# A linear-attention and MoE kernel on one core: exclusive sums by subtraction, some transposes by DMA, the first weight matrix in four loads, and a new order

## The chip, the cores and the metric

The kernel runs on one core of a Trainium2 chip. The metric is the time of one execution on the device, in microseconds (us), lower is better. Most executions of one kernel agree within a per cent or so. An execution more than 1.5% above the fastest of the same kernel is called slow, and only fast ones are compared. TensorE does matmuls (its weight loads are listed apart and run beside the matmuls), VectorE (DVE), ScalarE (ACT) and GpSimd (POOL) do elementwise work, and the queue of SyncE (SP) issues most of the DMAs.

## The reference

Two operations in a row. The first is a linear attention with a decay per channel and a bonus u for the current token; the second is a two-layer MLP with a tanh gelu (called MoE here, with one expert).

```python
# r, k, v, w: (4, 8, 768, 48); u: (8, 48); w_in: (384, 2048); w_out: (2048, 384)
state = zeros((B, H, D, D))
for t in range(S):
    cur = einsum('bhd,bhe->bhde', u[None] * k_t, v_t)
    y[:, :, t] = einsum('bhd,bhde->bhe', r_t, state + cur)
    state = w_t[:, :, :, None] * state + einsum('bhd,bhe->bhde', k_t, v_t)
x = y.transpose(0, 2, 1, 3).reshape(B * S, H * D)
h = x @ w_in
g = 0.5 * h * (1 + tanh(c * (h + 0.044715 * h**3)))      # c = sqrt(2 / pi)
out = g @ w_out
```

## The kernel before

The sequence is cut into 12 units (3 windows of 256 tokens by 4 batches); a partition holds a pair of tokens, and one unit has two chunks of 64 pairs. A unit goes through: loads of r, k, v, w; logarithm of w; cumulative sums on TensorE; exponentials; scaling of k and r; their transposes; the scores (tiles mt, then masked into sc); y; the state; the MoE matmuls h and o. All of it is laid out by hand: one long string of words is the program order of every engine at once. A word is a step, with the unit, the PSUM banks after @, and the engine as the last letter.

```python
ORDER = """
const.3.D load.w.0 clr.S.1.D ... ln.2 cum.2@35 kw.2.P y.1.0@24 ... load_wout.0 ... rka.2.P ...
"""

def cum(q, e):                       # units 2 to 11
    lw = logws[q % NLW]
    z = bank([P, 512], FP, f"z{q}")
    PE.matmul(z[:, 0:HD], incl, lw[:, :, 0:D], start=True, stop=True)     # inclusive sum
    ...                              # 4 small matmuls: the sum of a whole chunk
    x = bank([P, 512], FP, f"x{q}")
    PE.matmul(x[:, 0:HD], strict, lw[:, :, 0:D], start=True, stop=True)   # exclusive sum
    st["z", q], st["x", q] = z, x

def Td(q, wh, e):                    # transposes of kk (wh 0) and rq (wh 1) by DMA, most units
    src = (kks[q % NKK], rqs[q % NRQ])[wh]
    dst = buf(f"T{wh}", q, 2, [P, 2, G, 2, 64], BF)
    for c2 in range(2):
        SP.dma_start(out=dst[:, c2]..., in_=src[ds(64 * c2, 64)]..., transpose=True)

def X(q, c2, e):                     # MoE input: 3 transposes per chunk, through a permutation
    ...                              # that also puts the two tokens of a pair back in order
    for cb in range(NCB):
        PE.transpose(st["Xp", q][:, c2, cb, :], xt[:, ts(cb, P)], perm...)

def Xc(q, e):                        # and their evacuation from PSUM
    t = buf("xT", q, 2, [P, 2, NCB, P], BF)
    ...

def mm1(q, i, e):                    # h: 6 matmuls of 256 columns
    ...
    w_t = w_in_sb[i * NWI // 8][:, cb, ds(i * 2 * P % (DF // NWI), 2 * P)]
    w_t = w_t.rearrange("p (m s) -> p s m", s=WOP)[:, f, :]     # WOP = 2: every second column

def gl(q, i, e):
    t = buf(f"g{i}", q, NG, [P, 2, WIN], BF)
    ACT.activation(out=t, in_=st.pop(("h", q, i)), func=AF.Gelu_apprx_tanh)
```

## Time and profile before

| | before |
|---|---|
| median of the three runs at the start | 183.63 us (182.74 to 185.92; the highest is slow) |
| span of the profiled run | 181.3 us |
| first h matmul at | 23.1 us |
| from the start of the first h matmul to the end of the last o matmul (the body) | 154.5 us |
| from there to the end (the tail) | 3.7 us |

The three parts are read from the matmuls in the trace. The prediction below shows the page and the chain of this run; two rows of the page's groups of instructions complete it. A row reads: line, engine, operation, output<-input, shape, count, then busy time in us and mean duration in ns, then the idle time of the engine before them.

```profile
L566 ACT ACTIVATE g<-h 128x512 bf16<-128x512 f32 x96 | 52.2, 600 | 24.7 <-PE h L560 24.1
L560 PEld LDWEIGHTS <-w_in_sb 128*128 128x128 bf16 x576 | 55.6, 98 | 9.5
```

All 96 gelus take 600 ns, the weight load of h takes 98 ns, and ScalarE idles before gelus because it waits for TensorE, not the other way round.

### The profile page before, as it was taken

The numbers are of one execution on the slowest core, as the hardware profiler recorded it, in microseconds if no ns is written. First come the engines' busy times: TensorE is split into PE (matmuls) and PEld (weight loads), VectorE is DVE, ScalarE is ACT, GpSimd is POOL, SyncE is SP. The second block draws the span as 40 slices with busy tenths as digits, with TensorE's granted clock in tenths as the row PEclk, the third lists the DMA queues.
The fourth block names the chain that finished last, engine by engine and source line by source line (L and its number), as shares of the span: only waits on it lengthen the run. The fifth ranks groups of instructions, "written<-read, shape, count | busy, mean of one in ns | idle before, by whom it ended". The sixth has DMA issues, their size and how long they took to land.

```text
span 181.3 us, 5364 instructions
## 1 busy us (share of the span) xinstructions
PE 175.4 (97%) x2237; PEld 128.9 (71%) x2237; DVE 106.7 (59%) x218; ACT 118.5 (65%) x221; POOL 111.1 (61%) x115
## 2 busy tenths in 40 slices
PE   7999899999999999999999999999999999999991
PEld 4367689866786698767866777867856776887660
DVE  3279996644689853583598885385094876720010
ACT  2679688774777698686973788865864924344721
POOL 8599899568989597527999999955066400000000
PEclk9999999999999999999999999999999999999999
DMA  5999999999999996999899885687754453021004
GB/s 148 261 261 238 262 232 233 247 248 235 213 173 208 277 204 96 269 275 248 81 278 297 169 232 105 175 189 84 189 150 87 79 93 113 0 86 48 0 22 151
DMA packets 73753, 31.53 MB, mean 174 GB/s; under 512 B 68865, under 2 KB 72962, under 8 KB 73730
## 3 DMA queue, kind: packets, MB, share of 16 engines
q1 hardware_dynamic: 71152, 27.08, 69.9%
q0 software_dynamic: 1856, 3.15, 9.4%
q10 hardware_dynamic: 722, 0.98, 1.6%
q8 instruction: 17, 0.28, 0.7%
q14 instruction: 6, 0.05, 0.1%
HBM read 25.17 MB, written 4.72 MB: 165 GB/s over the span
## 4 chain that ended last, share of the span: by engine, by line
PE 88%; POOL 3%; DMA 3%; DVE 1%; issue 1%; ACT 1%; SPq 1%; POOLq 0%
PE o L573 35%; PE h L560 35%; PE mt L459 4%; DMA k<-in_k_dram 3%; PE y L481 3%; PE y L524 2%; PE p L494 2%; PE Xp L541 2%; POOL rk L403 2%; PE z L323 1%; PE x L328 1%; POOL rk L409 1%; PE T L380 1%; DVE sc L466 1%; PE dummy L276 1%
## 5 line engine op out<-in xcount | busy, mean ns | idle before, releaser
L573 PE MATMUL o<-w_out_sb,g 128*128 128x384 bf16 x384 | 73.0, 326 | 0.0
L560 PE MATMUL h<-xT,w_in_sb 128*128 128x256 bf16 x576 | 69.5, 273 | 0.0
L566 ACT ACTIVATE g<-h 128x512 bf16<-128x512 f32 x96 | 52.2, 600 | 24.7 <-PE h L560 24.1
L560 PEld LDWEIGHTS <-w_in_sb 128*128 128x128 bf16 x576 | 55.6, 98 | 9.5
L573 PEld LDWEIGHTS <-g 128*128 128x128 bf16 x384 | 35.5, 98 | 18.5
L466 DVE CAST_PREDICATED sc<-mask,mt 128x512 bf16<-128x512 uint16 x48 | 30.0, 685 | 15.4 <-PE mt L459 15.3
L420 POOL TENSOR_TENSOR sc<-eye,dg 128x512 bf16<-128x512 bf16 x20 | 20.7, 1044 | 15.1 <-DVE dg L414 15.0
L403 POOL TENSOR_TENSOR rk<-k,u_bc 128x768 f32<-128x768 f32 x12 | 21.8, 1816 | 2.3 <-DMA k<-in_k_dram 2.2
L409 POOL TENSOR_TENSOR rk<-rk,r 128x768 f32<-128x768 f32 x12 | 21.8, 1818 | 0.2
L414 DVE TENSOR_REDUCE dg<-rk 128x16 f32<-128x768 f32 x12 | 11.4, 950 | 9.4 <-POOL rk L409 9.3
L582 DVE COPY ob<-o 128x384 f32<-128x384 f32 x11 | 6.1, 555 | 16.6 <-PE o L573 16.5
L515 DVE TENSOR_TENSOR s<-p,al 64x192 bf16<-64x192 f32 x40 | 14.2, 354 | 2.9 <-PE p L494 2.0
L353 POOL TENSOR_TENSOR rw<-r,w 128x384 f32<-128x384 f32 x10 | 10.0, 1001 | 8.8 <-DMA r<-in_r_dram 8.8
L531 ACT ACTIVATE xs<-y 128x384 bf16<-128x384 f32 x20 | 9.5, 489 | 8.0 <-PE y L524 5.4
L507 DVE TENSOR_TENSOR p<-p,s 64x192 f32<-64x192 f32 x32 | 11.7, 367 | 3.8 <-PE p L494 2.8
L580 ACT ACTIVATE ob<-o 128x384 f32<-128x384 f32 x13 | 6.4, 492 | 9.1 <-PE o L573 8.2
L281 POOL TENSOR_TENSOR ww<-w 128x384 f32<-128x384 f32 x10 | 10.0, 1005 | 2.4 <-DMA w<-in_w_dram 2.3
L347 POOL TENSOR_TENSOR kw<-k,w 128x384 f32<-128x384 f32 x10 | 10.0, 1003 | 2.5 <-DMA k<-in_k_dram 2.5
L630 ACT ACT_TABLE_LOAD x8 | 10.3, 1283 | 1.4 <-PEq L647 1.3
L632 ACT ACT_TABLE_LOAD x8 | 10.3, 1283 | 0.1
L276 PE MATMUL dummy<-warm_src 128*128 128x256 bf16 x41 | 7.3, 329 | 1.2 <-DVE warm_src L221 1.1
L432 POOL CAST vb<-v 128x768 bf16<-128x768 f32 x9 | 7.4, 823 | 1.6 <-DMA v<-in_v_dram 1.6
(90 smaller groups left out, 183.7 us busy)
## 6 DMA issues: line engine op xcount, KB each, us to landing
w<-in_w_dram SPq DMA_DIRECT2D x12, 384.0 KB, 5.2
k<-in_k_dram SPq DMA_DIRECT2D x12, 384.0 KB, 6.2
r<-in_r_dram SPq DMA_DIRECT2D x12, 384.0 KB, 6.4
v<-in_v_dram SPq DMA_DIRECT2D x12, 384.0 KB, 5.8
out_dram<-ob SPq DMA_DIRECT2D x19, 192.0 KB, 3.7
w_in_sb<-in_moe_w_in_dram POOLq DMA_DIRECT2D x2, 768.0 KB, 9.1
w_out_sb<-in_moe_w_out_dram POOLq DMA_DIRECT2D x2, 768.0 KB, 9.8
out_dram<-ob ACTq DMA_DIRECT2D x5, 192.0 KB, 2.3
```

The lines of the kernel that those rows point to most:

```text
L403: ENG[e].tensor_tensor(out=t, in0=st["k", q].rearrange("p h (t d) -> p h t d", t=2), in1=u_bc[:, :, None, :].broadcast_to([P, H, 2, D]), o ...
L409: ENG[e].tensor_tensor(out=t, in0=t, in1=st["r", q].rearrange("p h (t d) -> p h t d", t=2), op=AL.mult)
L414: DVE.tensor_reduce(out=t, in_=st.pop(("rk", q)), axis=AX.X, op=AL.add)
L420: POOL.tensor_tensor(out=bass.AP(tensor=o.tensor, offset=o.offset, ap=[list(o.ap[0]), [256, 4], [192, 2], [1, 64]]), in0=eye[:, None, None ...
L466: DVE.copy_predicated(scs[q % NSC][n][:, :, j].rearrange("p a b c i -> p a (b c i)"), mask.rearrange("p a b t -> p (a b t)").bitcast(U16)[ ...
L507: DVE.tensor_tensor(out=p2[rows, :, cols], in0=p2[rows, :, cols], in1=s[rows, :, cols], op=AL.add)
L515: DVE.tensor_tensor(out=s[rows, :, cols], in0=p2[rows, :, cols], in1=st["al", q][rows, :, c2][:, :, None].broadcast_to([64, G, D]), op=AL. ...
L560: PE.matmul(h[:, f, :], w_t, xt[:, :, cb, :], start=(f + cb == 0), stop=(cb == NCB - 1), skip_group_check=True)
L566: ACT.activation(out=t, in_=st.pop(("h", q, i)), func=AF.Gelu_apprx_tanh)
L573: PE.matmul(st["o", q, c2], st["g", q, i][:, f, ts(c2, P)], w_out_sb[i * NWO // 8][:, (2 * i + f) % (NFT // NWO), :], start=(i + f == 0), ...
L630: ACT.preload_act_table_set(EXP_SET)
L632: ACT.preload_act_table(AF.Gelu_apprx_tanh)
```

## The change

Four things at once. For units 2 to 11 the exclusive sum is no longer a matmul but the inclusive sum minus its own last term, on VectorE. For units 7, 9, 10 and 11 the MoE input is transposed by DMA; the DMA transpose used here does not permute tokens, so the gelu of those units writes its output in a strided order. w_in comes in four DMAs instead of two, and the weights' column step grows from 2 to 4. The same constant, WOP, also sets how many rows of w_out lie side by side in a partition, so that load changes too: its packets are 1024 of 1536 bytes before and 512 of 3072 after. The order string is new throughout.

```diff
-NWI = 2
+NWI = 4
-WOP = 2
+WOP = 4
+XSUB = 1
 ... (ORDER: all words in a new sequence; one place that matters later:)
-... kw.2.P ... load_wout.0 ... rka.2.P ...
+... rka.2.P ... load_wout.0 ... kw.2.P ...
 ... (in cum:)
-        x = bank([P, 512], FP, f"x{q}")
-        PE.matmul(x[:, 0:HD], strict, lw[:, :, 0:D], start=True, stop=True)
-        st["z", q], st["x", q] = z, x
+    def xd(q, e):
+        x = bank([P, 512], FP, f"x{q}")
+        DVE.tensor_tensor(out=x[:, 0:HD].rearrange("p (h d) -> p h d", d=D),
+                          in0=st["z", q][:, 0:HD].rearrange("p (h d) -> p h d", d=D),
+                          in1=logws[q % NLW][:, :, 0:D], op=AL.subtract)
+        st["x", q] = x
 ...
+    def Xd(q, c2, e):
+        if ("xT", q) not in st:
+            st["xT", q] = buf("xT", q, 2, [P, 2, NCB, P], BF)
+        SP.dma_start(out=st["xT", q][:, c2], in_=st.pop(("xs", q, c2)), transpose=True)
+        by_dma.add(q)
 ... (in gl:)
-        ACT.activation(out=t, in_=st.pop(("h", q, i)), func=AF.Gelu_apprx_tanh)
+        h = st.pop(("h", q, i))
+        if q in by_dma:
+            ACT.activation(out=t.rearrange("p f (c i s) -> p (f c) s i", c=2, s=2),
+                           in_=h.rearrange("p f (c s i) -> p (f c) s i", c=2, s=2),
+                           func=AF.Gelu_apprx_tanh)
+        else:
+            ACT.activation(out=t, in_=h, func=AF.Gelu_apprx_tanh)
```

## The prediction

> **What bounds the kernel now.** I read four things in this order: the engine shares and slices of the page, the waits of TensorE, the chain of work that ended last, and the groups by line. First the page:
>
> ```profile
> PE 175.4 (97%) x2237; PEld 128.9 (71%) x2237; DVE 106.7 (59%) x218; ACT 118.5 (65%) x221; POOL 111.1 (61%) x115
> PE   7999899999999999999999999999999999999991
> DMA  5999999999999996999899885687754453021004
> ```
>
> TensorE is busy 97% of the span, and every slice between the first five and the last is full. A busy TensorE is not proof of a full one, since the ends of matmuls are modelled and overlap, so I look at what it waited for. Its own list of waits is two lines long:
>
> ```profile
> PE dummy L276 <- DVE warm_src L221: 1.1, 1, 1.1
> PE y L524 <- issue: 0.5, 1, 0.5
> ```
>
> Both lie in the first 21 us. Later no matmul waits for another engine. The chain says the same in time order:
>
> ```profile
> 1.86 5.77 DMA k<-in_k_dram
> 7.78 1.82 POOL rk L403
> ...
> 15.63 1.21 DVE sc L466 x2
> 16.88 1.05 PE dummy L276 x8
> ...
> 22.99 0.28 PE y L524 x4
> 23.27 1.31 PE h L560 x12
> ...
> 152.45 0.17 PE Xp L541 x3
> ...
> 154.76 1.31 PE h L560 x12
> ...
> 169.46 8.14 PE o L573 x50
> 177.59 0.02 issue
> 177.62 0.49 ACT ob L580
> ```
>
> There are three parts. A head of 23.3 us to the first real MoE matmul runs through load, GpSimd and VectorE, and TensorE fills it with dummy matmuls. A body of 154.3 us is TensorE matmul after matmul. A tail of 3.7 us follows: the copy of 0.49 us, the store and the close. The chain also gives the true rates, which the mean durations hide: 12 h matmuls of 256 columns in 1.31 us are 109 ns each, 3 Xp transposes of 128 columns in 0.17 us are 56 ns. The 50 o matmuls of 384 columns in 8.14 us are 163 ns each. The rows that the change touches, by form:
>
> ```profile
> L541 PE MATMUL Xp<-perm,xs 128*128 128x128 bf16 x72 | 6.5, 219 | 0.0
> L328 PE MATMUL x<-logw,strict 128*128 128x384 bf16 x10 | 3.2, 322 | 0.0
> ```
>
> Their busy sums (6.5 and 3.2 us) overstate them about twofold: a mean of 219 ns holds a pipeline latency that the next matmul overlaps.
>
> **What the Trainium skill says.** "TensorE: Matmul & The Clock Gate", section "Back-to-back issue gap", gives N/2.4 + 2.5 ns for the isolated warm gap of N columns: 56, 109 and 163 ns for 128, 256 and 384. The trace agrees with all three. The same page, "Weight-path perf modes", says that the fast weight load of 128 non-fp32 weights allows a column step of up to about a thousand elements. The change reads w_in with a step of 4 where before it was 2; this trace has a mean load of 98 ns at step 2 and also at step 1 (g), and none at step 4. "VectorE: DVE Perf Modes", "The perf-mode tier table", puts a tensor_tensor with an operand in PSUM at 1x, so 384 columns are 384/0.96 = 400 ns and some set-up; the trace has 0.55 us for rq and kk of that shape. "DMA: Bandwidth & Descriptors", "Issuing engines are not separate DMA queues", says that all issuers share the same 16 engines; I use it for the loads of the head, where the DMA row stands at 9.
>
> **The change, part by part.**
> 1. Exclusive sums. For units 2 to 11 the strict matmul goes: 10 x 163 ns = 1.63 us off the body (unit 2's stands in the head, so 9 of them, 1.47 us, are certain). In its place VectorE subtracts logw from z: 10 x 0.55 us = 5.5 us on an engine that is at 59%. Exp of x now waits for z, then for the subtraction, so rq is some 0.5 us later per unit, and z in PSUM is held longer. The searched order puts other matmuls in between.
> 2. Transposes by DMA for units 7, 9, 10 and 11: 4 x 6 x 56 ns = 1.34 us of TensorE go, and with them four evacuations of 0.56 us (VectorE) or 0.81 us (ScalarE). Eight DMA transposes come in on SP. The existing ones occupy SP for about 1.26 us each and land after a median 3.0 us; each moves 128 KB, the new ones 98 KB, so about 1 us and 3 us. SP has room after 100 us, where the DMA row falls to 7 and below. Adding the rates above along the new order of TensorE, the slack for unit 11 is about 12 us of matmuls between the last a5 and mm1, for a path of 0.6 + 0.6 + 3 us; unit 9 has about 3 us after its second transpose. I see no stall there.
> 3. The gelu write with a stride of two elements: 32 of 96 gelus. Same element count, so I keep 0.60 us each; even 0.75 would add 4.8 us to a ScalarE at 65%.
> 4. w_in in four DMAs, the first some 6 us earlier: in the before trace a w_in half is issued at 11.89 us and lands 9.1 us later. The same bytes in all. Each quarter takes about 2 us of the DMA engines, estimated from the first half's roughly 4 us burst at 15 to 19 us. The first quarter now falls among the loads of k and r of unit 1.
> 5. The head. VectorE sets it: from its first evacuation of T at 11.6 us it works almost without a pause up to the decay of s at 22.7 us, which releases the last y and then h. The changed head has the same VectorE operations there. It can start about 0.5 us earlier, since unit 0's evacuation no longer follows a longer chain of exps, but k of unit 1 now comes at about 12.5 us by the load rates (1.5 us per load, plus the quarter of w_in), which takes it back. I count 0 to +0.5, say +0.2 us. Five more dummies (46 for 41) lie in idle time.
> 6. The tail: the last copy and store stay on ScalarE. Three other copies and two stores stand ahead of them there now, at 0.49 and 0.34 us; counted back from the last o matmul they just fit. 0 us.
>
> Sum: -1.6 - 1.3 + 0.2 = -2.7 us. I add 0.2 us for waits that a new order has on a chip and not on paper. With 183.6 before, that gives **181.1 us**, a gain of 1.4%.
>
> **The rivals.**
> - A new wait in the body, because rq comes later and the loads have been reordered (v of unit 3 now comes behind two transposes on SP). For it: the DMA row is at 9 through half the span, and one load issue held SP for 5.1 us. Against it: TensorE has 10 us and more of MoE matmuls of units 0 and 1 to run while unit 2 and 3 are prepared, and before shows no such wait. It would give 182 to 184 us.
> - The head grows, because w_in quarters and loads collide: the first h would start at 24.5 to 25.5 and take back half of the gain, 182 to 183.5 us. For it: the software queue takes most of the DMA bandwidth while it runs. Against it: the first half's worth of w_in is no longer ahead of r of unit 2.
> - The weight load at step 4 is slower than 109 ns and becomes the bound of 576 matmuls: 20 ns more each would be 11 us, about 192 us. For it: only 11 ns lie between 98 and 109. Against it: step 1 and step 2 cost the same 98 ns, and the skill's limit is far off.
> - The new order is also better elsewhere: the 1.1 us and 1.4 us that h and o take beyond their rates in the body go, and the head shortens by 0.5. That would be 179 us. The body has no more than these 2.5 us to give, as nothing in it waits.
>
> **Range and chances.** The part that I trust is the 2.7 to 3.0 us of TensorE work. Head and waits are uncertain by a microsecond to each side, more upward, as a saturated TensorE leaves little downward; the times before spread over 182.7 to 185.9. So 8 times in 10 within **179.4 to 183.4 us**. Faster by over 2% is a time under about 180.0 (or under 179.6, if the runs before come out as the lower two did), which needs the last rival in part: 0.2. Slower by over 2% needs the third rival, or a stall of over 6 us: 0.03. Within 2%: 0.77.
>
> **What would show it.** Right: TensorE loses 10 strict matmuls and 24 transposes, h keeps 109 ns and its weight load 98 ns, TensorE's list of waits stays empty after the first h, the first h starts at 22.8 to 24 us, and the body shortens to about 151.5 us; the gelus with the strided write stay at 0.60 us. Wrong: waits of TensorE for DMA, VectorE or ScalarE in the body, a first h after 24.5 us, a weight load over 105 ns, or a tail over 4 us. If the time falls under 179.5 us with a body of over 151 us, the head gave more than I allow.

## The result and the profile after

| | before | after |
|---|---|---|
| median, first pair of runs | 183.38 us (6 runs, one of them slow) | 181.41 us (6 runs, one of them slow) |
| ratio, fast runs | 1 | 0.9899, 95% interval 0.9869 to 0.9928 |
| the same kernels again in a later batch | 183.63 us (11 runs, two slow) | 182.95 us (6 runs, one slow) |
| ratio there | 1 | 0.9954, 0.9911 to 0.9997 |
| profiled run: span | 181.3 us | 180.1 us |
| profiled run: first h, body, tail | 23.1, 154.5, 3.7 us | 23.4, 153.1, 3.7 us |

A ratio is the mean time of one kernel's fast runs over the mean of the other's fast runs of the same rounds, so it is not quite the ratio of the medians quoted beside it. By the 2% measure the two kernels are the same; the change gains about 0.7% (the mean of 0.990 and 0.995), or 1.4 us. Where a text below says "the changed kernel's 0.993", it is this mean.

The page of the changed kernel, the lines that answer to those shown of before:

```profile
PE 172.5 (96%) x2208; PEld 134.0 (74%) x2208; DVE 112.1 (62%) x232; ACT 131.6 (73%) x225; POOL 112.7 (63%) x115
...
PE   7998999999999999999997999999899999999991
...
L578 PEld LDWEIGHTS <-w_in_sb 128*128 128x128 bf16 x576 | 62.1, 114 | 3.9
...
L590 ACT ACTIVATE g<-h 128x512 bf16<-128x512 f32 x64 | 34.7, 606 | 4.6 <-PE h L578 3.6
...
L586 ACT ACTIVATE g<-h 128x512 bf16<-128x512 f32 x32 | 21.6, 766 | 15.0 <-PE h L578 15.0
...
L654 ACT ACT_TABLE_LOAD x13 | 16.7, 1283 | 1.5 <-PEq L671 1.3
```

TensorE lost 2.9 us of busy time and 29 instructions net (10 matmuls and 24 transposes fewer, 5 dummies more). Two slices of its row in the body, which were full, are now at 7 and 8. ScalarE went from 118.5 to 131.6 us: the strided gelus take 766 ns instead of about 606, and there are 26 loads of activation tables (13 in the row shown and 13 in one beside it) where before had 16. The Trainium skill, "ScalarE: Activation LUTs", section "What ACT_TABLE_LOAD costs", gives about 1283 ns for one such load, which the trace shows to the nanosecond; ten more are 12.8 us. The loads were not foreseen, the slower gelus only as a fallback. Neither set the end in this run: ScalarE still idles before these gelus because TensorE has not made h yet.

The waits of TensorE in the changed kernel (who waited <- for whom: us in all, times, longest):

```profile
PE mt L471 <- DMA T<-rq: 1.1, 2, 0.9
...
PE p L506 <- POOL vb L444: 0.6, 1, 0.6
```

The kernel before had no wait in the body. These two are in it. The chain of waits around them shows where each comes from (start, duration, what; SPq is the issue of a DMA):

```profile
91.73 5.37 DMA T<-rq
...
97.15 0.64 PE mt L471 x31
...
118.37 1.27 SPq L408
...
119.74 0.53 SPq L249
...
120.31 5.92 DMA v<-in_v_dram
...
126.36 0.83 POOL vb L444
...
127.23 0.50 PE p L506 x8
```

The DMA transpose of rq of unit 7 is issued at 91.7 us and takes 5.4 us to land; the scores wait for it. Later, v of unit 10 is issued at 120.3 us, after the issue of four transposes has held SyncE one behind the other from 113.6 to 119.6 us (the 1.27 us of SPq is the last of them) and the issue of another load another 0.5 us. It lands 5.9 us later, is cast by GpSimd, and only then the p matmuls run.

The gaps between starts of matmuls, less the rate of each kind, are 1.05 us and 0.40 us at the first place and 0.73 us at the second: 2.2 us. Nine strict matmuls and 24 transposes in the body are 9 x 163 + 24 x 56 ns = 2.8 us less work. The body is 1.4 us shorter. So the rest of the new order won 1.4 - (2.8 - 2.2) = 0.8 us. By the same count of gaps, 0.4 us of it is in the intervals after h matmuls, which run closer to their rate; those after o matmuls do not, and the rest lies among the small matmuls.

The first of these waits is not the work of the new DMA transposes. In the time line of SyncE the first of them is issued at 105.9 us, when the scores of unit 7 have already waited at 96.7 us. The place of unit 7's own transposes in the new order is the likelier cause: e1 and e2 below move one of them, and the wait for rq goes (but it is missing from the one profiled run of e3 too, which moves nothing). The old order missed the same wait narrowly: the last transpose of unit 7 landed at 103.1 us there, and its scores began at 103.5 us. Before the load of v of unit 10, two new transposes do stand in the queue (105.9 and 111.7 us).

### The profile page after: what moved, and what is told of

Read it like the earlier page. It is cut to its first block, busy times and chain, and to the rows that moved or that the text cites. A ratio compares the mean times of both kernels' runs of the same rounds, so it can differ in the third digit from the quotient of the medians.

```text
span 180.1 us, 5345 instructions
## 1 busy us (share of the span) xinstructions
PE 172.5 (96%) x2208; PEld 134.0 (74%) x2208; DVE 112.1 (62%) x232; ACT 131.6 (73%) x225; POOL 112.7 (63%) x115
## 4 chain that ended last, share of the span: by engine, by line
PE 85%; DMA 6%; DVE 3%; SPq 1%; issue 1%; ACT 1%; POOL 0%; POOLq 0%
PE o L597 33%; PE h L578 30%; DMA v<-in_v_dram 3%; PE mt L471 3%; DMA T<-rq 3%; PE y L493 3%; PE dummy L279 3%; PE p L506 2%; PE y L536 2%; PE T L392 1%; PE Xp L553 1%; PE m L295 1%; SPq L408 1%; PE u_ps L260 1%; DVE rq L383 1%
## 5 line engine op out<-in xcount | busy, mean ns | idle before, releaser
L578 PE MATMUL h<-xT,w_in_sb 128*128 128x256 bf16 x576 | 70.9, 273 | 0.0
L578 PEld LDWEIGHTS <-w_in_sb 128*128 128x128 bf16 x576 | 62.1, 114 | 3.9
L590 ACT ACTIVATE g<-h 128x512 bf16<-128x512 f32 x64 | 34.7, 606 | 4.6 <-PE h L578 3.6
L586 ACT ACTIVATE g<-h 128x512 bf16<-128x512 f32 x32 | 21.6, 766 | 15.0 <-PE h L578 15.0
L654 ACT ACT_TABLE_LOAD x13 | 16.7, 1283 | 1.5 <-PEq L671 1.3
L656 ACT ACT_TABLE_LOAD x13 | 16.7, 1283 | 0.2
L543 ACT ACTIVATE xs<-y 128x384 bf16<-128x384 f32 x14 | 7.0, 505 | 5.5 <-PE y L536 3.7
L604 ACT ACTIVATE ob<-o 128x384 f32<-128x384 f32 x15 | 7.1, 487 | 3.7 <-PE o L597 3.7
L471 PE MATMUL mt<-T,T 48*64 48x128 bf16 x384 | 8.1, 219 | 1.1 <-DMA T<-rq 1.1
```

The source lines that it names most:

```text
L471: PE.matmul(ms[j][ds(64 * c2, 64), gi, t2, :], kT[ds(64 * j, D), c2, g, t2, :], rT[ds(64 * j, D), c2, g, :, :], start=(gi + t2 == 0), stop ...
L578: PE.matmul(h[:, f, :], w_t, xt[:, :, cb, :], start=(f + cb == 0), stop=(cb == NCB - 1), skip_group_check=True)
L586: ACT.activation(out=t.rearrange("p f (c i s) -> p (f c) s i", c=2, s=2), in_=h.rearrange("p f (c s i) -> p (f c) s i", c=2, s=2), func=AF ...
L590: ACT.activation(out=t, in_=h, func=AF.Gelu_apprx_tanh)
L654: ACT.preload_act_table_set(EXP_SET)
L656: ACT.preload_act_table(AF.Gelu_apprx_tanh)
```

## The experiments

Twelve kernels ran, in three batches, each batch on one chip with its own runs of the kernel before, five timed rounds each. All but the two marked wrong gave the right result. The changed kernel with edits is meant unless a text says otherwise.

| run | edit | median us | ratio to before | body, profiled run |
|---|---|---|---|---|
| e1_both_waits | two words moved to take away both waits | 182.13 | 0.9937 | 153.4 |
| e2_wait_a | the first of them only | 182.43 | 0.9929 | 155.1 |
| e3_x_on_pe | exclusive sum as a matmul again | 183.07 | 0.9978 | 155.7 |
| e4_X_on_pe | MoE inputs transposed on TensorE again, first try | 185.85 | 1.0137 | 157.9 |
| c_after | none (control) | 182.95 | 0.9954 | 154.2 (slow) |
| e4c_X_on_pe_clean | as e4, other banks | 183.95 | 0.9994 | 153.6 |
| e9_unit7_pe | unit 7 alone on TensorE again | 183.15 | 0.9960 | 155.0 |
| e5_wop2 | weight step 2 | 184.09 | 0.9998 | 153.8 |
| e7_before_sub | the kernel before with the subtraction alone | 184.60 | 1.0074 | 155.6 |
| e10_best | e4c mended, with the word of e2 moved | 183.09 | 1.0000 | 154.1 |
| e11_half_loads | half the bytes of later loads (wrong) | 180.99 | 0.9867 | 153.1 |
| e6_gelu_plain | contiguous gelu write (wrong) | 181.29 | 0.9883 | 153.1 |

The intervals of the ratios are 0.003 to 0.006 to each side, those of a difference between two ratios are wider, and only the second batch ran the changed kernel itself as a control. A difference of less than that proves nothing alone.

### The two waits: e1 and e2

```diff
 e1 and e2:  -load.w.9 ... Td.7.0 ... load.v.7 ... Td.7.1
             +Td.7.1 load.w.9 ... Td.7.0 ... load.v.7
 e1 also:    -p.10@1 mm2.7.1.4 ... mm2.7.0.4
             +mm2.7.1.4 ... mm2.7.0.4 p.10@1
```

> The changed kernel with two moves in the order: the second transpose of rq of unit 7 goes to SP ahead of three loads (it stood behind them and the transpose of kk), and the p matmuls of unit 10 go five o matmul pairs later on TensorE. Theory: TensorE's work sets the body, and two waits (1.5 us of issue gap at mt of unit 7, 0.75 us at p of unit 10) took back most of what the removed matmuls gave. Both gaps go: 179.2 to 179.9 us, ratio to before about 0.979. Rival (the transfers limit the middle, so a transpose that goes first only makes a load late and the wait turns up elsewhere): 180.8 to 181.5 us, ratio 0.987 to 0.99, with new waits of TensorE.

> Only the first of the two moves (transpose of rq of unit 7 ahead of three loads). Theory: -1.5 us against the changed kernel, 179.7 to 180.2 us, ratio 0.981; the wait at p of unit 10 stays at 0.7 us. Rival (a saved wait is lost again at the next one, which is set by a load): the wait at p grows by what was saved, and the time stays at 181.2 to 181.6 us.

(The edit of e1 moves the p matmuls behind four o pairs, not five.) Neither is faster than the changed kernel's 0.993, and both intervals exclude the theory's 0.979 and 0.981. In e1 both waits are gone, but others stand in their place, for the transposes of kk (0.8 us in all); e2, with the first wait gone, shows the wait for vb at 1.2 us, twice what it was, and a new one of 1.4 us for w_out, which the edit does not touch. The waits of TensorE in e1, then in e2:

```profile
PE mt L467 <- DMA T<-kk: 0.8, 2, 0.5
```

```profile
PE o L594 <- DMA w_out_sb<-in_moe_w_out_dram: 1.4, 1, 1.4
PE p L503 <- POOL vb L441: 1.2, 1, 1.2
```

The gaps in the body come to 2.1 us in e1 by the count used above, against 2.2 in the changed kernel: the stall goes from one transfer to another, and the time does not fall. That is the mechanism of the rivals, though the medians, 182.13 and 182.43 us, lie above their ranges.

### What each part is worth in the new order: e3, e4, e4c, e9, e10

```diff
 e3 (in xd):
-        DVE.tensor_tensor(out=x[:, 0:HD]..., in0=st["z", q]..., in1=logws..., op=AL.subtract)
+        PE.matmul(x[:, 0:HD], strict, logws[q % NLW][:, :, 0:D], start=True, stop=True)
 e4, e4c, e10 (ORDER, units 7, 9, 10, 11; e9: unit 7 only):
-Xd.7.0 ... Xd.7.1
+X.7.0@5 X.7.1 Xc.7.D            (e10: @3 and a little later; e4: @4, Xc.7.A)
 e10 also: mm2.6.1.5 and mm2.6.1.6 before mt.8.1, and Td.7.1 before load.w.9
```

> The changed kernel, with the exclusive sums of units 2 to 11 as the strict matmul again, at the same place of the order and in the same bank. Theory (saturated TensorE): 9 x 163 ns come back in the body and part of the tenth in the head: +1.4 to +1.6 us, 182.8 to 183.1 us. Rival (the subtraction costs in waits on VectorE and ScalarE about what it saves): 0 or less, 181.2 to 181.6 us.

e3 came out at 0.9978, 0.5% or 0.95 us above the changed kernel's mean. The matmuls that came back are 1.5 us of the body. The interval of e3 is 0.8 us to each side, and against the two measurements of the changed kernel it is 1.5 and 0.4 us slower, so the direction agrees with the theory and the size is open. Its profiled run also drew a wait of 1.7 us for vb; the edit changes nothing in that load's path, but whether it plays a part is not shown.

> The changed kernel, with the transposes of the MoE inputs of units 7, 9, 10 and 11 on TensorE again with their evacuations, and the plain gelu write for them. Theory: 24 x 56 ns come back: +1.3 us, and up to 0.5 us for the new evacuations in a dense order: 182.6 to 183.2 us. Rival (the eight DMA transposes hold SP and the queue, and so cause the wait for the transpose of rq and the late load of v): without them the waits shrink, and the time stays or falls, 180.5 to 181.5 us.

This run is a miss: at 1.0137 it says little of the transposes. In the trace the transposes took bank 4 and their evacuation went to ScalarE, late; the subtraction of unit 10 needed that bank, the masks stand behind it in VectorE's order and came late, and h waited 1.7 us for them. The second try puts the tiles in other banks.

> The changed kernel again, unaltered, as the control of this batch: 181.4 us, ratio 0.99 against the kernel before.

> The changed kernel with the MoE inputs of units 7, 9, 10 and 11 transposed on TensorE again, in banks chosen so that no bank is waited for (this mends what was wrong with the earlier such run). If the DMA transposes are worth what the count says (24 transposes of 56 ns, 1.34 us, minus the 0.7 to 1.5 us of waits that their place in the queue brings), this is 0 to +1.3 us against the control. Rival, that the eight DMA transposes cost the DMA queue more than they give TensorE: it is faster than the control by 0.5 us or more, and the waits for the transposed rq of unit 7 and for v of unit 10 are below 0.3 us.

> Only unit 7 back on TensorE (6 transposes, +0.34 us of TensorE); units 9, 10 and 11 stay on DMA, where fewer loads are left. The issue stream is freed of the two transposes that stood in front of the load of v for unit 10 (2.0 and 1.2 us), so that load should be issued about 2 us earlier and the wait of the p matmuls for vb should vanish (0.6 to 0.7 us). Theory (queue position makes the wait): -0.3 us against the control. Rival (transfer rate, not position, makes it): +0.3 us, with the wait still there.

> The changed kernel with the subtraction kept, no MoE input transposed by DMA, unit 7's in a bank that is free by then (the earlier clean version waited 0.7 us for a gelu there), and the DMA transpose of rq of unit 7 issued before the load of w for unit 9. If the DMA transposes bring nothing because their queue gives the time back, this is as fast as the changed kernel or faster: 0.985 to 0.992 against before, no wait in the body above 0.4 us, body 152.5 to 153.3 us. If they are worth their 1.3 us, it is slower than the changed kernel: 0.996 to 1.000.

The control came out at 0.9954, half a per cent above the first pair: this is how far the same kernel moves from one batch to another. Beside it, e4c is 0.4% slower, 0.7 us, inside both intervals; e10, with its banks mended, is at 1.0000, 1.4 us above the changed kernel's mean. That this is near the 1.34 us of the 24 transposes is partly chance: its profiled run also drew a gap of 1.0 us for w_out (see below) and one of 0.7 us for masks that stood on VectorE behind the evacuation of the transposes. Neither run is faster, as the rival asked, so what the DMA transposes cost the queue is not more than they save; how much of the 1.34 us is left is open. e9 is as fast as the control (0.9960). The wait for vb is not in its profiled run, as the theory said, but it is not in that of e6 below either, whose SyncE has all eight transposes, so this does not show the queue position as its cause. The wait for rq of unit 7 stayed (1.2 us in all). e10 was meant to beat both kernels and does not.

### The subtraction alone in the old order: e7

```diff
 (kernel before, in cum)
-        PE.matmul(x[:, 0:HD], strict, lw[:, :, 0:D], start=True, stop=True)
+        DVE.tensor_tensor(out=x[:, 0:HD]..., in0=z[:, 0:HD]..., in1=lw[:, :, 0:D], op=AL.subtract)
```

> The kernel before with one part of the change alone: the exclusive sum of units 2 to 11 made by a VectorE subtraction, in the old order, everything else as before. Theory (TensorE is the bound and the old order has the slack): 10 matmuls of 163 ns leave, -1.6 us, ratio 0.991, VectorE busy +5.7 us (10 x 0.57). Rival (the matmuls that stay now wait for VectorE or for transfers as they do elsewhere): ratio 0.998 to 1.002, with new waits on VectorE or on loads of over 0.5 us.

Ten matmuls leave TensorE, and the kernel becomes 0.7% slower (1.0036 to 1.0112), worse than the rival said. The chain of waits shows why. Before, at the same place (scores, cumulative sum, MoE matmuls, y):

```profile
103.52 0.66 PE mt L459 x32
...
105.18 0.18 PE x L328
105.36 0.97 PE o L573 x6
...
107.32 0.51 PE y L481 x32
```

and in e7:

```profile
104.18 0.36 PE mt L461 x14
...
105.17 1.28 DVE sc L468 x2
...
106.48 0.58 DVE x L328
...
107.14 0.06 ACT x L339
...
107.52 0.49 ACT ob L582
...
108.06 0.56 PE y L483 x31
```

Before, TensorE is its own chain. In e7 the chain leaves TensorE: masks on VectorE, then the subtraction (0.58 us) behind them, then the exponential on ScalarE that waits for it, then the copy of o that stands behind the exponential on ScalarE and frees the bank of y. At 94, 108 and 122 us y starts later than its rate allows, by 0.3 to 0.5 us each time; with the smaller gaps elsewhere in the body it comes to 2.5 us, more than the 1.6 us saved. An engine at 59% has room on average and none at the moment when it counts. So what the subtraction gains in the changed kernel, it gains together with the order that was made for it.

### The gelu write and the weight step: e6 and e5

```diff
 e6 (in Xd):  -        by_dma.add(q)
 e5:          -WOP = 4
              +WOP = 2
```

> Wrong token order on purpose: the changed kernel with a contiguous gelu write in all units. The 32 gelus of units 7, 9, 10 and 11 fall from 766 to about 606 ns (5.1 us less on ScalarE); as ScalarE is not the bound, time within 0.3 us of the changed kernel (0.990 to 0.995 against before). Rival (the longer gelu holds banks and h): over 0.7 us faster than the changed kernel, ratio 0.986 or below.

> The changed kernel with the weights of the first MoE matmul read at a step of 2 again, as before (one constant; w_in still in four DMAs). Theory (the slower weight loads are hidden under the matmuls): mean weight load of that line back from 114 to 98 ns, time within 0.3 us of the control. Rival (they bound the h matmuls): 576 loads times 16 ns, up to 0.5 us or more faster.

The two groups in question, in e6 and then in e5:

```profile
L590 ACT ACTIVATE g<-h 128x512 bf16<-128x512 f32 x96 | 52.3, 607 | 21.9 <-PE h L578 21.0
```

```profile
L578 PEld LDWEIGHTS <-w_in_sb 128*128 128x128 bf16 x576 | 55.3, 98 | 9.8
```

So the strided write costs 160 ns a gelu and the step of 4 costs 16 ns a weight load. The traces show both hidden: the body of e6 is as long as that of the changed kernel, 153.1 us, and the h matmuls keep their 109 ns at either step. The times do not contradict it: e6 is at 0.9883 (0.9822 to 0.9943), not clearly apart from the changed kernel's 0.9899 and 0.9954, though this interval does not exclude its rival, and e5 at 0.9998 is not faster. That e5 is slower than its control by 0.4% is within the intervals; its profiled run drew the wait for w_out explained below, in which its edit may have a part.

### The bytes: e11

```diff
 (in load; tiles kept across units so that the rest holds older data)
-        SP.dma_start(out=t, in_=... ap=[[2 * D, P], [S * D, H], [1, 2 * D]])
+        n = H if q < 4 else H // 2
+        SP.dma_start(out=t[:, 0:n], in_=... ap=[[2 * D, P], [S * D, n], [1, 2 * D]])
```

> Wrong result on purpose: the changed kernel, but the loads of r, k, v, w from unit 4 on fetch half the heads (the other half keeps older data); same instructions, same order. Theory (the rate of transfers in the middle sets when rq of unit 7 and v of unit 10 are there): the body's waits for them (1.05, 0.40 and 0.73 us) vanish, body 151.0 to 151.8 us, ratio 0.975 to 0.985. Rival (the issue order on the one issuing engine sets it, whatever the bytes): the waits stay, within 0.3 us of what they were, ratio 0.990.

Same instructions, same order, fewer bytes (26.0 MB moved for 32.3). The waits for rq of unit 7 and for v of unit 10 are gone from the list: the transpose that took 5.4 us landed in 3.6 us, and the load of v that took 5.9 us in 3.2 us. So the bytes in flight had a part in these waits and not the issue order alone; it is one profiled run, and e3 and e6 lack one of the two waits each with all bytes. But the body is 153.1 us, not 151.0 to 151.8, and the ratio of 0.9867 is 0.6% below the changed kernel's mean and not apart from e6 (0.9883), which ran on the same chip. The theory's 0.975 to 0.985 lies below it, though the interval (0.9830 to 0.9904) reaches the upper end. What TensorE waits for longest in the body of e11:

```profile
PE o L599 <- DMA w_out_sb<-in_moe_w_out_dram: 1.1, 2, 0.7
```

It stalled there for 0.55 and 0.87 us beyond the rates; without that the body would be 151.7 us, in the expected range (arithmetic, no run).

### A wait that comes and goes

The wait for w_out is in 6 of the 12 profiled runs of the changed kernel and its variants outside e7 (e2, e4, e5, e9, e10, e11: 0.8 to 1.7 us) and not in the others, though their programs up to there hardly differ. Where it comes from can be read on GpSimd, which issues this load in two halves. The time line of GpSimd in the changed kernel, then in e2, then in the kernel before (start, duration, what, and in brackets the idle time before and what ended it):

```profile
23.40 1.83 POOL L415 TENSOR_TENSOR rk<-k,u_bc 128x768 f32<-128x768 f32 x1
25.17 0.76 POOL L272 DMA_DIRECT2D w_out_sb<-in_moe_w_out_dram  x1
...
30.27 0.76 POOL L272 DMA_DIRECT2D w_out_sb<-in_moe_w_out_dram  x1
```

```profile
25.49 1.82 POOL L412 TENSOR_TENSOR rk<-k,u_bc 128x768 f32<-128x768 f32 x1 [2.28 <-DMA k<-in_k_dram]
27.26 0.76 POOL L269 DMA_DIRECT2D w_out_sb<-in_moe_w_out_dram  x1
...
32.34 0.76 POOL L269 DMA_DIRECT2D w_out_sb<-in_moe_w_out_dram  x1
```

```profile
23.38 1.01 POOL L347 TENSOR_TENSOR kw<-k,w 128x384 f32<-128x384 f32 x1 [0.30 <-DMA k<-in_k_dram]
24.32 0.81 POOL L269 DMA_DIRECT2D w_out_sb<-in_moe_w_out_dram  x1
25.15 1.83 POOL L403 TENSOR_TENSOR rk<-k,u_bc 128x768 f32<-128x768 f32 x1
```

In both orders the first half stands behind a product that needs k of unit 2: before it is kw (1.0 us), in the new order the longer rk (1.8 us). What differs besides is k itself: SyncE issues it at 13.4 us before and at 15.0 us in the new order. In e2 k came 2.3 us late, so both halves were issued 2.1 us later than in the changed kernel; the second follows the first by 5.1 us in every run of the new order. What TensorE waits for is the half that lands after its o matmuls are due: in e2, e4 and e10 the second (at 42.0 to 42.7 us), in e5 and e9 the first (at 36.6 and 36.7), in e11 both. In the runs without the wait the second half landed at 41.1 us or earlier. e5 has a reason of its own: at step 2 the six halves in three traces (before, e7, e5) took 9.7 to 10.4 us to land, at step 4 those of the fast runs took 7.9 to 10.2, with a median of 9.1. So this load is where the step of 4 may help; no run separates it from the step of w_in. Half of the runs by 1.2 us is an estimated 0.6 us for the mean time. Moving the word load_wout.0 ahead of rka.2.P could take away the wait for the first half; the second stands behind three more products of GpSimd and would have to be moved as well. That was not tried and stays open.

## Why the prediction was right or wrong, point by point

The time, 181.1 us, was close in the first pair, 181.4 us, and less so in the later batch, 182.95 us. Both lie within 179.4 to 183.4 us and both are the same by the 2% measure, but that range reaches up to the time before (183.38 us), so to lie in it says little. The body tells more: it was to shorten to about 151.5 us and came to 153.1.

- **Removed work** (-1.6 and -1.3 us). Right in count and mechanism: 10 matmuls and 24 transposes less, and the two undone separately cost 0.95 us (e3) and 0.7 to 1.4 us (e4c, e10), each with an interval of about 0.8 us to each side. Wrong as a sum of independent parts: the subtraction alone in the old order costs 1.4 us (e7). "The searched order puts other matmuls in between" was the condition of the term, not a remark beside it.
- **No new wait in the body.** This step failed. "I see no stall there" looked at the slack between xs and h for the new transposes; that held, and no h waited for a transposed MoE input in the profiled run. But TensorE waited for what shares their queue: rq of unit 7, before any new transpose was issued, so not through them, and v of unit 10, with two of the new transposes ahead of it, 2.2 us of gaps in all. The sizes behind the step were off too. A new transpose was to hold SyncE for about 1 us; they hold it for 1.2 us and more (2.0 us for unit 7's first). And "the DMA row falls to 7 and below" after 100 us misreads the row shown: it stands at 8 to 109 us and again from 118 to 122 us, and in the changed kernel at 9 again from 122 to 131 us. The first rival had named this cause (transfers reordered on SyncE) and argued it away with the MoE matmuls that TensorE could run meanwhile. In a fixed order TensorE cannot run them meanwhile unless the order says so.
- **+0.2 us for waits.** The term that was mis-sized: 2.2 us in the profiled run. It was partly made up by 0.8 us elsewhere, the part of the last rival that came true. That these errors partly cancelled was luck.
- **The head**, +0.2 us: first h at 23.4 after 23.1, right in the first pair. What the second rival said of the software queue (GpSimd's) can be read from the trace before: from 16 to 19 us it moved 0.56 MB, SyncE's queue 0.06 MB. The wait for w_out after the head was not seen; the load depends on k of unit 2 in both orders, and k is issued 1.6 us later in the new one.
- **The gelu stays at 0.60 us**: wrong, 766 ns; the fallback of 0.75 us in the same sentence was the better number. Harmless, as said: e6.
- **The weight load stays at 98 ns**: wrong, 114 ns. The third rival feared that a load slower than 109 ns would become the bound; the load did become slower than 109 ns and h still runs 12 matmuls in 1.31 us in the chain. So a mean duration of the weight load is not its interval, just as with the matmuls. e5 shows no gain from undoing it, though it also changes the load of w_out.
- **The tail**, 0 us: right, 3.69 after 3.67 us.

What stays open: whether the new transposes make the wait for v of unit 10, how much of the 0.5% between the two measurements of the changed kernel is the wait for w_out, and whether an order without it reaches the 179 us that the last rival set.

## What to carry to other kernels

Work taken off a saturated engine counts at its issue interval, but only if the replacement fits the moment: check what stands behind it in the order of its new engine, not that engine's average load. When DMAs are added, look at what lies behind them in their queue, and at which loads are issued behind an instruction that itself waits for a load; such a load inherits the arrival time of another. A wait seen in one profiled run may not be there in the next, so a wait should be read in several runs before an order is rearranged for it.

## What the Trainium skill lacked or had wrong

- "TensorE: Matmul & The Clock Gate", section "Weight-path perf modes", gives a range of column steps within which the fast weight load works, but no cost inside it: steps 1 and 2 take 98 ns (384 and 576 loads), step 4 takes 114 ns (576 loads), without effect on h at 109 ns.
- "ScalarE: Activation LUTs" has no figure that I found for a strided bf16 output: 128x512 with a stride of two elements took 766 ns, contiguous 606 ns. Its 1283 ns for a table load agrees.
- "DMA: Bandwidth & Descriptors" says who may issue DMA transposes, but how long one holds the issuing queue only in cycles and for other sizes, in a comparison of chips: in the time line of SyncE here, 2.0 us and 1.2 us for the two of unit 7's MoE input, in which no later load of that queue is issued.
- No page that I read says how far the landing of a load moves between runs of programs that are the same up to there (here perhaps on different chips): GpSimd waited 2.28 us for k of unit 2 in e2 and not at all in the changed kernel, against a whole effect of 1.4 us.
